# Three mixtures in one kernel: the products with V one item behind, and a spill that is kept in two parts

## The chip, the cores and the metric

One core of a Trainium2 chip runs the whole program. The metric is the device time of one execution in microseconds (us), as the median of the runs given below. Five engines work side by side, each taking its own instructions in the order of its queue: TensorE (PE; its weight loads are listed apart as PEld), VectorE (DVE), ScalarE (ACT), GpSimd (POOL) and SyncE (SP), which here only issues transfers. ACT and POOL issue transfers too.

## The reference, cut to what matters

```
scores = q @ k.T / sqrt(64)                 # 4 batches, 8 heads, 768 tokens, 64 wide
keep   = key among the first 4, or one of the last 128 up to the query
a      = softmax(where(keep, scores, -1e9)) # attention, then  x = a @ v  as 3072 x 512
h      = max(x @ w1, x @ w2, x @ w3)        # first mixture, 768 wide
x2     = h @ w_out                          # 3072 x 512
logits = x2 @ w_gate                        # 8 experts, at most 384 tokens each,
                                            # best (token, expert) bids first
out    = relu(x2 @ W1[e]) @ W2[e]           # second mixture, per token's expert e
```

## The kernel before

The 3072 tokens are cut into eight groups of 384 (half a batch each), numbered 0 to 7. A group's attention is four items (units), one for each pair of heads; item p of group g is written a<g>.<p> below. An item has four steps in class Attn: `load` issues its transfers on SP's queue; `prep` splits k, q and v into two float32r parts, of which one is the value rounded and the other what was left (items of groups 0 and 1 are computed in float32 and need no such split); `score` makes twelve products in PSUM tiles `ps`, copies them into the tile T (ACT, L134) and masks them (DVE, L130 to L137); `soft` takes the maxima (DVE, L141), the exponentials (ACT, L144), and scales T (POOL, L147). Then `pv` transposes T on TensorE (`flip`, L25, into `pt` and `pp`), masks the transposes (DVE, L163), splits them (ACT L176, POOL L177), multiplies with V (TensorE, L181 and L182, into `po`) and writes the item's result tile x (ACT L183, DVE L184; L173 for the float32 items).

The first mixture, class Moe1, works through the groups. `group` first splits a group's four x into the tiles `xh0` to `xh3` and `xl0` to `xl3` (ACT L267, DVE L268; one buffer each), then makes for each of six slices f three times twelve products (L280), takes their maximum into `hm` (ACT L282, DVE L283) and splits this into the parts h and l (ACT L288, DVE L289), which lie in the tile HL. `x2` multiplies these with w_out, 108 products of 260 columns (L305), and writes x2 to memory. Group 0 comes before w_out has been unpacked: its `hm` is written to memory as it is (ACT's queue, L285), and after group 1's x2 `reload` brings each slice back into `hm` (SP's queue, L321), splits it (ACT L323, DVE L324) into HL, and group 0's x2 follows. The eight groups are followed by the routing of the tokens and the second mixture.

Three things set the order of the instructions. First the order in which the program writes them: the lists `order` and `order1` and, from group 2 on, `between(f)`, which emits an item of the next group ahead of slices 0, 1, 3 and 4. Second a scheduler that takes them in order of priority, each as soon as its model of the engines lets it; items of later groups are lifted by 60 instructions (`off`), evictions of PSUM to the front. Third the buffers: x0 to x3, `xh`, `xl`, `pt`, `pp` and `po` have one each, T has three, `mm` and `hm` two. Tiles `st` (two buffers in the pool `conv`) hold words of w_out before they are unpacked in `load_out` (L220 to L228).

Of the kernel before, what the change touches and what calls it, by code (L numbers as in the profile page):

```python
# [19 lines left out]
FT=mybir.dt.float32; FR=mybir.dt.float32r; BF=mybir.dt.bfloat16; I32=mybir.dt.int32; U8=mybir.dt.uint8; U32=mybir.dt.uint32  # L20
AF=mybir.ActivationFunctionType; OP=mybir.AluOpType; AX=mybir.AxisListType
NEG=-8.0e9
def f32(ap): return ap.bitcast(FT)
# [179 lines left out]
class Moe1:  # L203
# [56 lines left out]
    def group(s,xs,spill=None,pool=None,mid=None,between=None):  # L260

        nc=s.nc; main=s.main
        X=[]
        for p in range(4):
            h=main.tile([128,384],FR,name=f"xh{p}",bufs=1); l=main.tile([128,384],FR,name=f"xl{p}",bufs=1)
            with s.tc.high_priority():
                nc.scalar.activation(h,xs[p],AF.Copy)  # L267
                nc.vector.tensor_tensor(l,xs[p],f32(h),op=OP.subtract)  # L268
            X.append((h,l))
        H=[]  # L270
        if s.HL is None and spill is None: s.HL=main.tile([128,12,384],FR,name="HL")
        for f in range(6):
            if between is not None: between(f)
            m=main.tile([128,384],FT,name="hm",bufs=2)
            for i in range(3):
                ps=s.mm.tile([128,512],FT,name="mm")
                n=0
                for p in range(4):
                    for a,b in ((0,0),(0,1),(1,0)):
                        nc.tensor.matmul(ps[:,:384],s.W[i][a][:,p,f*128:(f+1)*128],X[p][b],start=(n==0),stop=(n==11)); n+=1  # L280
                with s.tc.high_priority():
                    if i==0: nc.scalar.activation(m,ps[:,:384],AF.Copy)  # L282
                    else: nc.vector.tensor_tensor(m,ps[:,:384],m,op=OP.max)  # L283
                if mid is not None and (f,i)==s.at: mid()
            if s.HL is None: nc.scalar.dma_start(spill[f],m); continue  # L285
            h,l=(pool.tile([128,384],FR,name=f"h{x}{f}",bufs=1) if pool else s.part(x,f) for x in "hl")
            with s.tc.high_priority():
                nc.scalar.activation(h,m,AF.Copy)  # L288
                nc.vector.tensor_tensor(l,m,f32(h),op=OP.subtract)  # L289
            if spill is not None:  # L290
                for d,x in zip(spill[f],(h,l)): nc.scalar.dma_start(d,f32(x))
            H.append((h,l))
        return H
# [21 lines left out]
                nc.scalar.activation(LG[:,t0+t,:].rearrange("p (u e) -> p u e",u=2),e,AF.Copy)  # L315
            nc.scalar.dma_start(x2d[(t0+t)*128:(t0+t+1)*128,:],o)
    def reload(s,spill):
        nc=s.nc; H=[]
        for f in range(6):
            m=s.main.tile([128,384],FT,name="hm",bufs=2)  # L320
            nc.sync.dma_start(m,spill[f])  # L321
            h,l=s.part("h",f),s.part("l",f)
            nc.scalar.activation(h,m,AF.Copy)  # L323
            nc.vector.tensor_tensor(l,m,f32(h),op=OP.subtract)  # L324
            H.append((h,l))
        return H
    def by_rows(s,spill,t0,x2d,accs,pool):

# [28 lines left out]
class Route:  # L357
# [4 lines left out]
    M=128  # L362
# [261 lines left out]
def attention_mixtures(tc,q,k,v,vs,words,wg,u1,u2,out,off=60,spread=(0,1,3,4),native=8,order='a0 a0 a0 a0 w a1 w a1 w w a1 w w a1 a2',order1='a2 o o o o o o a2 a2',back=1,at=(1,0),s1=300,s2=400,nring=6):  # L624
    nc=tc.nc
    PS=bass.MemoryType.PSUM
    with ExitStack() as ctx:
# [6 lines left out]
        x2d=dram.tile([3072,512],FT,name="x2d")  # L634
        A=Attn(tc,q,k,v,vs,consts,ac,pst,psp,pss,psv,work)
        M=Moe1(tc,words,wg,consts,wpool,main,conv,mm,pst,pss,A.ident)
        M.at=at
        LG=consts.tile([128,24,8],FT,name="LG")
        NG=8; xs={}; cnt={}
        def att(g,p):  # L640
            xs.setdefault(g,[])
            u=A.load(g//2,g%2,p,4*g+p<native); A.prep(u); A.score(u); A.soft(u)
            x=main.tile([128,384],FT,name=f"x{p}")
            A.pv(u,x); xs[g].append(x)
        def lw(f): M.load_w(f)
        def lo(f): M.load_out(f)
        with tc.block(schedule_with_timeline_sim=True):
            A.extra=Spare(main)
            A.kf=[A.zeros([A.extra.tile([128,4,132],FT,tag=f'kf{i}{h}') for h in range(2)]) for i in range(3)]
            def emit(o,p):  # L650
                n=cnt[o]=cnt.get(o,-1)+1
                if o[0]=='a':
                    if p:
                        with tc.high_priority(offset=off): att(int(o[1:]),n)
                    else: att(int(o[1:]),n)
                elif o=='w': lw(n)
                else:
                    A.extra=None; lo(n)
                    if n==5:
                        conv.release()  # L660
                        A.extra=A_("extra",1,side="right"); A.no=('A',)
                        A.kz.append(A.zeros([A.extra.tile([128,4,132],FR,name=f'kz{h}b') for h in range(2)]))
            for o in order.split(): emit(o,False)
            rest=None
            for g in range(NG):
                if g==1:
                    for o in order1.split(): emit(o,True)
                late=list(range(cnt.get(f'a{g+1}',-1)+1,4)) if g+1<NG else []
                def between(f):
                    if f in spread and late: late.pop(0); emit(f'a{g+1}',True)  # L670
                if g<2:
                    while late: between(spread[0])
                d = g>=NG-3
                if g==0: sp=[dram.tile([128,384],FT,name=f"sp{f}") for f in range(6)]
                if g==NG-3: sp2=[[dram.tile([128,384],FT,name=f"sp{f}{x}") for x in "hl"] for f in range(6)]
                if g==NG-1:
                    A.extra.release(); work.release(); ac.release(); psv.release(); pss.release(); psp.release()
                    acc=P("acc",1,space=PS); rc=P("rc",2,space=PS)
                    rt=P("rt",1); rw=P("rw",2); hp=A_("hp",1)
                    r=Route(tc,LG,rt,rw,rc)  # L680
                H6,H=H if g==NG-1 else None,M.group(xs[g],sp if g==0 else sp2 if g==NG-3 else None,hp if g==NG-1 else None,rest,between)
                while late: between(spread[0])
                rest=None
                if d:
                    rest=M.logits(H,3*g,LG)
                    if g==NG-1: r.bids((0,21),True)
                elif g: M.x2(H,3*g,LG,x2d)
                if g==back:
                    M.x2(M.reload(sp),0,LG,x2d)
# [6 lines left out]
        def fet(n):  # L696
            G.append([E.fetch(S[n][0],None if n else T7*128),S[n][1],S[n][0]])
# [22 lines left out]
            P7=[main.tile([128,384],FR,name=f"x{j}") for j in range(3)]  # L720
            for j in range(3): nc.vector.tensor_scalar(P7[j],io,r.q[:,T7+j:T7+j+1],None,op0=OP.is_equal)
        M.x2(H6,T7-3,LG,x2d,256,hp)
        M.by_rows(sp2,T7-6,x2d,acc,hp)
        with tc.high_priority(): fet(0)
        M.x2(H,T7,LG,x2d,256,hp,keep)
        hp.release()
# [62 lines left out]
```

## Time and profile before

| what | value |
|---|---|
| median of 3 runs | 993.31 us (990.75 to 993.98) |
| the profiled execution: its own time | 985.81 us |
| its span, first to last instruction | 984.0 us |
| PE, PEld, DVE, ACT, POOL busy | 937.8, 857.8, 687.8, 533.8, 348.8 us |
| mean granted TensorE clock | 0.977 |

The rows come from one profiled execution, whose own time is 7.5 us under the median of the other runs; a sum of changes is made against it. "Busy" of PE counts pipelined matmuls to their modelled ends, so the weight loads (PEld) show more plainly where TensorE has nothing to do. A granted clock of 1.0 is 2.4 GHz; the lower level is 1.2 GHz, and a value in between is a mix of the two over a stretch.

### The profile page before, as it was taken

How to read it: one execution, taken by the hardware profiler on the slowest of the kernel's cores; microseconds unless marked ns; L12 is line 12 of the kernel's file. 1: busy time of each engine (PE TensorE's matmuls, PEld its weight loads, DVE VectorE, ACT ScalarE, POOL GpSimd, SP SyncE). 2: the span in 40 equal slices, each digit the busy share in tenths (PEclk: the TensorE clock that was granted, in tenths of full speed). 3: DMA queues.
4: the chain of work that ended last, by engine and by line, in shares of the span. 5: the costliest groups of instructions: out<-in, count | busy, mean ns of one | idle time of the engine just before them, and what ended most of it. 6: DMA issues, size and time to landing. Idle time of an engine off the chain costs nothing.

```text
span 984.0 us, 18469 instructions
## 1 busy us (share of the span) xinstructions
PE 937.8 (95%) x6552; PEld 857.8 (87%) x6552; DVE 687.8 (70%) x1807; ACT 533.8 (54%) x1425; POOL 348.8 (35%) x317
## 2 busy tenths in 40 slices
PE   5889999969999999999999999999999999999996
PEld 4568989959999999999999998888888888888895
DVE  3897676687879976776764344879989889873320
ACT  4666664788789777677663211233433434344431
POOL 3578357145555535425434000011113032043331
PEclk8899999989999999999999999999999999999999
DMA  7455121222112112112110002544345352454420
GB/s 226 151 170 172 50 77 64 68 83 88 53 40 78 52 49 73 28 48 81 64 50 12 1 1 76 164 154 130 119 149 174 98 172 99 160 189 154 135 81 32
DMA packets 50541, 95.03 MB, mean 97 GB/s; under 512 B 6704, under 2 KB 20784, under 8 KB 50448
## 3 DMA queue, kind: packets, MB, share of 16 engines
q1 hardware_dynamic: 40560, 71.57, 23.4%
q0 software_dynamic: 3840, 12.45, 3.6%
q10 hardware_dynamic: 6048, 9.83, 2.7%
q8 instruction: 51, 0.84, 0.4%
q14 instruction: 42, 0.34, 0.1%
HBM read 77.84 MB, written 16.12 MB: 95 GB/s over the span
## 4 chain that ended last, share of the span: by engine, by line
PE 75%; DVE 8%; ACT 6%; issue 5%; DMA 4%; POOL 1%; SPq 1%; POOLq 0%; ACTq 0%; DVEq 0%
PE mm L280 28%; PE mm L608 11%; PE acc L601 11%; PE mm L305 7%; PE po L181 3%; PE rc L406 2%; PE pt L25 2%; PE pp L25 2%; PE po L172 2%; PE ps L126 1%; PE ps L127 1%; DMA sa<-in_u_dram 1%; PE ps L123 1%; DVE A_w L163 1%; DVE qs L97 1%
## 5 line engine op out<-in xcount | busy, mean ns | idle before, releaser
L601 PE MATMUL acc<-wbh,HL 128*128 128x512 f32 x384 | 131.1, 398 | 0.0
L177 POOL TENSOR_TENSOR L<-A_w,H 128x768 fp32r<-128x768 f32 x46 | 87.0, 1891 | 101.5 <-ACT H L176 91.1
L283 DVE TENSOR_TENSOR hm<-mm,hm 128x384 f32<-128x384 f32 x96 | 53.3, 555 | 68.6 <-PE mm L280 65.1
L620 POOL DMA_INDIRECT out_dram<-og,idx x24 | 32.2, 1340 | 180.6 <-ACT og L619 177.3
L305 PE MATMUL mm<-woh,HL 128*128 128x260 f32 (+1 forms) x432 | 89.5, 296 | 2.0 <-DVE HL L324 1.1
L552 ACT ACTIVATE wah<-sa 128x512 fp32r<-128x512 f32 x64 | 40.5, 632 | 89.6 <-PE mm L608 72.2
L601 PEld LDWEIGHTS acc<-wbh,HL 128*128 128x128 f32 x384 | 71.5, 188 | 12.8
L552 ACT ACTIVATE wbh<-sb 128x512 fp32r<-128x512 f32 x64 | 40.4, 631 | 74.9 <-PE acc L601 72.0
L601 PE MATMUL acc<-wbl,HL 128*128 128x512 f32 x192 | 76.9, 401 | 0.0
L305 PEld LDWEIGHTS mm<-woh,HL 128*128 128x128 f32 x432 | 72.3, 198 | 3.3 <-DVE HL L324 1.4
L608 PE MATMUL mm<-HL,wah 128*128 128x384 f32 x256 | 68.5, 343 | 0.0
L280 PE MATMUL mm<-xh,w0h 128*128 128x384 f32 x192 | 66.8, 348 | 1.2 <-ACT xh L267 0.6
L280 PE MATMUL mm<-xh,w1h 128*128 128x384 f32 x192 | 66.7, 347 | 0.8 <-ACT hm L282 0.5
L280 PE MATMUL mm<-xl,w0h 128*128 128x384 f32 x192 | 65.5, 341 | 1.9 <-DVE xl L268 1.9
L280 PE MATMUL mm<-xh,w2h 128*128 128x384 f32 x192 | 67.0, 349 | 0.0
L280 PE MATMUL mm<-xh,w1l 128*128 128x384 f32 x192 | 65.5, 341 | 0.0
L280 PE MATMUL mm<-xl,w2h 128*128 128x384 f32 x192 | 65.5, 341 | 0.0
L553 DVE TENSOR_TENSOR wbl<-sb,wbh 128x512 fp32r<-128x512 f32 x64 | 43.9, 688 | 30.7 <-ACT wbh L552 30.7
L280 PE MATMUL mm<-xl,w1h 128*128 128x384 f32 x192 | 65.1, 339 | 0.0
L280 PE MATMUL mm<-xh,w0l 128*128 128x384 f32 x192 | 65.1, 339 | 0.0
L280 PE MATMUL mm<-xh,w2l 128*128 128x384 f32 x192 | 65.1, 339 | 0.0
L612 DVE SCALAR_TENSOR_TENSOR HL<-mm,HL 128x384 fp32r<-128x384 f32 x64 | 35.5, 554 | 40.8 <-ACT HL L611 40.6
(320 smaller groups left out, 2888.3 us busy)
## 6 DMA issues: line engine op xcount, KB each, us to landing
sa<-in_u_dram SPq DMA_DIRECT2D x64, 256.0 KB
sb<-in_u_dram SPq DMA_DIRECT2D x64, 256.0 KB
HL<-in_words_dram SPq DMA_DIRECT2D x18, 512.0 KB
qn<-in_q_dram SPq DMA_DIRECT2D x24, 192.0 KB
x2d<-xo ACTq DMA_DIRECT2D x15, 256.0 KB
kn<-in_k_dram SPq DMA_DIRECT2D x12, 264.0 KB
st<-in_words_dram SPq DMA_DIRECT2D x6, 512.0 KB
vn<-in_v_dram SPq DMA_DIRECT2D x12, 256.0 KB
```

Source lines behind the costliest of these rows:

```text
L25: nc.tensor.transpose(out,x,f32(ident))
L177: nc.gpsimd.tensor_tensor(L,Af,f32(H),op=OP.subtract)
L181: nc.tensor.matmul(po[:,q:q+n],u['VS'][:,blk,128*h:128*h+128],part[:,c:c+n],start=(part is H and j==0),stop=False,skip_group_check=True)
L280: nc.tensor.matmul(ps[:,:384],s.W[i][a][:,p,f*128:(f+1)*128],X[p][b],start=(n==0),stop=(n==11)); n+=1
L283: else: nc.vector.tensor_tensor(m,ps[:,:384],m,op=OP.max)
L305: nc.tensor.matmul(ps[:,:n],H[f][a][:,t*128:(t+1)*128],s.WO[b][:,f,u,c],start=(k==0),stop=(k==17)); k+=1
L552: nc.scalar.activation(h,src,AF.Copy)
L553: (nc.gpsimd if s.n>=6 and nm=="wa" else nc.vector).tensor_tensor(l,src,f32(h),op=OP.subtract)
L601: s.mms.append(nc.tensor.matmul(acc[t],H[f][a][:,t*128:(t+1)*128],W[f][1][b],start=(f==0 and n==0),stop=(f==F-1 and n==2))); n+=1
L608: s.mms.append(nc.tensor.matmul(ps[:,:384],W[f][0][a][:,k,:],X[k][b],start=(n==0),stop=(n==11))); n+=1
L612: nc.vector.scalar_tensor_tensor(l,ps[:,:384],0.0,f32(h),op0=OP.max,op1=OP.subtract)
L620: st=nc.gpsimd.indirect_dma_start(out=s.out,out_offset=bass.IndirectOffsetOnAxis(ap=idx[:,t:t+1],axis=0),in_=o,in_offset=None)
```

## The change

An item's `pv` is no longer emitted with its other steps. `att` appends the item to a list, and `fin(keep, high)` emits the `pv` of the oldest items until `keep` remain. In `order`, one item is kept back among the four of group 0; from group 2's items on, one is kept back after each item, and none after an f or a `load_out` that emits no item. So the `pv` of an item stands behind the load, split, scores and softmax of the next.

Group 0's slices are split as they are made: h and l come from two buffers with the tag `st` of the pool `conv`, and both are written to memory (twelve transfers on ACT's queue instead of six). `reload` only issues twelve transfers on SP's queue: slices 0 to 3 into the tiles `xh0` to `xl3`, slices 4 and 5 into HL.

```diff
-            if s.HL is None: nc.scalar.dma_start(spill[f],m); continue
-            h,l=(pool.tile([128,384],FR,name=f"h{x}{f}",bufs=1) if pool else s.part(x,f) for x in "hl")
+            if s.HL is None: h,l=(s.conv.tile([128,2,384],FR,name="hp",tag="st",bufs=2)[:,x] for x in range(2))
+            else: h,l=(pool.tile([128,384],FR,name=f"h{x}{f}",bufs=1) if pool else s.part(x,f) for x in "hl")
...
     def reload(s,spill):
-        nc=s.nc; H=[]
+        H=[]
         for f in range(6):
-            m=s.main.tile([128,384],FT,name="hm",bufs=2)
-            nc.sync.dma_start(m,spill[f])
-            h,l=s.part("h",f),s.part("l",f)
-            nc.scalar.activation(h,m,AF.Copy)
-            nc.vector.tensor_tensor(l,m,f32(h),op=OP.subtract)
-            H.append((h,l))
+            H.append([s.main.tile([128,384],FR,name=f"x{x}{f}",bufs=1) if f<4 else s.part(x,f) for x in "hl"])
+            for d,x in zip(spill[f],H[f]): s.nc.sync.dma_start(f32(x),d)
         return H
...
+        pend=[]
         def att(g,p):
             xs.setdefault(g,[])
             u=A.load(g//2,g%2,p,4*g+p<native); A.prep(u); A.score(u); A.soft(u)
-            x=main.tile([128,384],FT,name=f"x{p}")
-            A.pv(u,x); xs[g].append(x)
+            pend.append((g,p,u))
+        def fin(keep,high):
+            while len(pend)>keep:
+                g,p,u=pend.pop(0)
+                with tc.high_priority(offset=off) if high else ExitStack():
+                    x=main.tile([128,384],FT,name=f"x{p}")
+                    A.pv(u,x); xs[g].append(x)
...
-            for o in order.split(): emit(o,False)
+            for o in order.split():
+                emit(o,False)
+                fin(int(o[0]=='a' and len(pend)+len(xs.get(0,[]))<4),False)
+            fin(0,False)
...
-                    for o in order1.split(): emit(o,True)
+                    for o in order1.split():
+                        emit(o,True); fin(int(o[0]=='a'),True)
+                    fin(0,True)
...
                 def between(f):
-                    if f in spread and late: late.pop(0); emit(f'a{g+1}',True)
+                    n=int(f in spread and len(late)>0)
+                    if n: late.pop(0); emit(f'a{g+1}',True)
+                    fin(n,True)
...
-                if g==0: sp=[dram.tile([128,384],FT,name=f"sp{f}") for f in range(6)]
-                if g==NG-3: sp2=[[dram.tile([128,384],FT,name=f"sp{f}{x}") for x in "hl"] for f in range(6)]
+                if g in (0,NG-3): sp=[[dram.tile([128,384],FT,name=f"sp{g}{f}{x}") for x in "hl"] for f in range(6)]
...
-                H6,H=H if g==NG-1 else None,M.group(xs[g],sp if g==0 else sp2 if g==NG-3 else None,hp if g==NG-1 else None,rest,between)
+                H6,H=H if g==NG-1 else None,M.group(xs[g],sp if g in (0,NG-3) else None,hp if g==NG-1 else None,rest,between)
                 while late: between(spread[0])
+                fin(0,True)
```

## Rows read from the trace of the kernel before

**Rows 1.** Stages: PE, PEld, DVE, ACT, POOL busy (instructions), clock, DMA share, GB/s.

```profile
0.00:64.00 64.00, 46.68 (x190) 31.24 (x190) 43.39 (x103) 38.83 (x136) 34.53 (x47) 0.87 0.61 189
64.00:125.00 61.00, 60.48 (x340) 53.93 (x341) 46.78 (x90) 38.54 (x120) 39.94 (x40) 0.97 0.35 115
...
199.00:236.50 37.50, 29.61 (x193) 27.42 (x194) 30.91 (x52) 33.04 (x99) 19.38 (x14) 0.82 0.28 85
236.50:300.00 63.50, 62.85 (x422) 61.88 (x420) 50.91 (x104) 51.93 (x156) 31.73 (x30) 1.00 0.18 52
300.00:557.00 257.00, 253.94 (x1692) 249.32 (x1692) 177.99 (x350) 173.32 (x495) 109.60 (x92) 1.00 0.16 50
557.00:984.00 427.00, 412.30 (x3230) 364.46 (x3227) 286.90 (x1005) 149.04 (x292) 81.05 (x68) 0.99 0.37 120
```

**Rows 2.** TensorE in order of time, 199 to 239 us: start, us, instructions, [idle before].

```profile
205.89 0.59 PE L126 MATMUL ps<-kh_x,qs 128*128 128x260 f32 x1 [2.00 <-DVE T_w L135]
...
206.49 0.42 PE L305 MATMUL mm<-woh,HL 128*128 128x260 f32 x1
...
208.70 0.80 PE L305 MATMUL mm<-woh,HL 128*128 128x260 f32 x2 [1.14 <-DVE HL L324]
...
217.83 0.39 PE L126 MATMUL ps<-kh_w,qs 128*128 128x260 f32 x1 [1.97 <-DVE T_w L135]
...
221.13 0.90 PE L25 MATMUL pp<-ident,T_w 128*128 128x128 f32 x3 [1.24 <-DVE A_w L163]
...
222.27 0.42 PE L305 MATMUL mm<-woh,HL 128*128 128x260 f32 x1
...
228.15 0.28 PE L305 MATMUL mm<-woh,HL 128*128 128x260 f32 x1
228.27 0.28 PE L305 MATMUL mm<-wol,HL 128*128 128x260 f32 x1
...
236.48 0.34 PE L280 MATMUL mm<-xh,w0h 128*128 128x384 f32 x1
```

**Rows 3.** The reload's instructions: count, ns least/median/most, first and last start.

```profile
L323 ACT ACTIVATE HL<-hm x6: 506/516/526, 196.3 to 213.2; 128x384 fp32r<-128x384 f32 x6
L324 DVE TENSOR_TENSOR HL<-hm,HL x6: 551/556/2194, 198.8 to 213.8; 128x384 fp32r<-128x384 f32 x6
...
L285 ACTq DMA_DIRECT2D sp<-hm x6: 326/326/341, 72.6 to 122.6; - x6
L321 SPq DMA_DIRECT2D hm<-sp x6: 320/327/334, 175.3 to 210.8; - x6
```

**Rows 4.** ScalarE in order of time, 200 to 300 us.

```profile
213.21 0.53 ACT L323 ACTIVATE HL<-hm 128x384 fp32r<-128x384 f32 x1 [1.60 <-DMA hm<-sp]
...
236.98 0.51 ACT L267 ACTIVATE xh<-x 128x384 fp32r<-128x384 f32 x1
...
293.84 1.77 ACT L267 ACTIVATE xh<-x 128x384 fp32r<-128x384 f32 x4
```

**Rows 5.** VectorE and GpSimd in order of time, 207 to 221 us.

```profile
207.41 3.35 DVE L324 TENSOR_TENSOR HL<-hm,HL 128x384 fp32r<-128x384 f32 x2
...
215.66 1.91 DVE L95 TENSOR_TENSOR kz0b<-kn,kh_x 64x528 fp32r<-64x528 f32 x1 [0.36 <-ACT kh_x L94]
...
220.12 0.96 DVE L163 TENSOR_TENSOR A_w<-pp,ul 128x768 f32<-128x768 f32 x1
...
208.19 2.15 POOL L177 TENSOR_TENSOR L<-A_w,H 128x768 fp32r<-128x768 f32 x1
```

**Rows 6.** TensorE in order of time, 23 to 65 us.

```profile
23.50 0.85 PE L25 MATMUL pt<-ident,T_w 128*128 128x128 f32 x3
...
64.52 0.44 PE L280 MATMUL mm<-xl,w0h 128*128 128x384 f32 x1 [1.10 <-DVE xl L268]
```

**Rows 7.** A transfer of w_out's words on SP, and ScalarE's first use of it.

```profile
135.86 0.33 SPq L220 DMA_DIRECT2D st<-in_words_dram  x1
...
140.22 0.68 ACT L226 ACTIVATE st<-st 128x512 int32<-128x512 uint32 x1 [2.26 <-DMA st<-in_words_dram]
```

More of the change, by code (lines that the diff above doesn't have):

```diff
@@ L722, in attention_mixtures @@
         M.x2(H6,T7-3,LG,x2d,256,hp)
-        M.by_rows(sp2,T7-6,x2d,acc,hp)
+        M.by_rows(sp,T7-6,x2d,acc,hp)
         with tc.high_priority(): fet(0)
```

## The prediction

> **What bounds the kernel now.** I read the shares by stage first, then TensorE in order of time where a stage is poor, then the instructions that end its waits, and last the queues of ScalarE, VectorE and GpSimd there. The reader should look in the first view for a stage in which weight loads (the second pair) fill less than the stage at a granted clock under 1.0. Up to 64 us TensorE is fed by transfers and by unpacking: loads fill 31.24 of 64 us. From 236.5 to 557 us it is nearly full: 61.88 of 63.5 and 249.32 of 257 us, at clock 1.00, so only 1.62 + 7.68 = 9.3 us are free there. The routing and the second mixture behind 557 us are not touched. One stage in the middle is poor: 199 to 236.5 us, 27.42 of 37.5 us at clock 0.82 [rows 1].
>
> What that stage loses: 37.5 - 27.42 = 10.1 us without a load. A mean of 0.82 between the levels 1.0 and 0.5 means 0.36 of the stage, 13.5 us, at 1.2 GHz; with the stage's own busy share of 0.73 that is 9.9 us of loads, which would have taken 4.9 us less at 2.4 GHz. Together 15.0 us, so the stage's work is 22.5 us at full clock. This is my scale for what a cure can give.
>
> In order of time one sees why. Group 0's x2, which works on the reloaded slices, starts at 206.49, waits 1.14 us for a reloaded slice's l at 208.70, and its second product begins only at 222.27, because TensorE's queue holds scores and transposes of items in between that wait for VectorE: 2.00, 1.97 and 1.24 us [rows 2]. VectorE was late because the reload's six subtractions lie there, one of 2.19 us against a median of 0.556 [rows 3], two of them with a span of 3.35 us, and because a split of k for a later item (1.91 us) comes ahead of the mask at 220.12 that frees `pp` [rows 5]. ScalarE itself waited 1.60 us for a transfer of the reload [rows 4]. Group 2's products follow at 236.48 [rows 2].
>
> **The reload.** Removed from the poor stage: six ACT copies of 0.516 us, 3.1 us, and six DVE subtractions, five at the median and one of 2.194, 5.0 us [rows 3]. ACT is the fuller of the two, 33.04 us of 37.5 [rows 1]; 29.9 us remain. If the stage stayed as full of ACT work as it is (0.88), it would last 34.0 us and the gain is 3.5; if ACT becomes gapless, 29.9 us and 7.6; if only TensorE counted, 22.5 us and 15.0. Nothing excludes 0, if another chain ends as late. I take 7.5: group 0's x2 no longer needs ACT and DVE, so TensorE has 108 products that are ready while the items' chains run, and a part of ACT's work here belongs to group 3's items and may slip. This also gives back clock, which falls here where TensorE waited and rises again once products run.
>
> Added in its place: twelve SP issues for six, 0.327 us each [rows 3]. Eight go into `xh`/`xl`, free once group 1's products end, and have group 1's whole x2 (108 products at 0.12 us, the distance of two such products, 13 us [rows 2]) to land. The four of slices 4 and 5 overwrite HL, so they wait for the last reads of group 1's x2. A transfer of the reload issued at 210.8 let ACT start at 213.21, 2.4 us [rows 3, 4]; four issues take 1.3 us, so slice 5 stands 3.7 us behind that last read. The first twelve products of group 0's x2 cover 1.4 us: up to 2.3 us uncovered, unless scores fill it. Queued behind these issues on SP are the next item's k and q. At the end, group 2's splits (0.51 us on ACT [rows 4], 0.556 on DVE as any such subtraction [rows 3]) must wait for `xh0` to be read for the last time, 15 products or 1.8 us before x2 ends; 1.1 us fits under that if both queues are free, and costs up to 1.1 us if not. I take +1.0 for both (0 to 3.4).
>
> **The split at group 0.** Six ACT copies (3.1 us), six more ACT issues of 0.326 us (2.0) and six subtractions (3.3) move to between 72.6 and 122.6 us [rows 3]. In that stage ACT has 61 - 38.54 = 22.5 us free and DVE 14.2, and TensorE is the full engine (PE 60.48 of 61) [rows 1]. So I take +0.5, with 0 and the whole 8.4 us as ends, the latter if no cover holds. Slots of `st` are taken until the last spill has landed, about 122.6 + 1.1 + 0.3 + 2.4 = 126.4 us; a load of w_out's words and its first use are 4.4 us apart [rows 7], so the second word comes at about 131 us, while group 0's and 1's x2 lie behind 175 us (the reload's first issue) [rows 3]. No cost, as long as six unpackings fit in 44 us.
>
> **One item behind.** No instruction is added; the queues' order changes. ACT, DVE and POOL work on the next item's scores and softmax ahead of the old item's splits, so the last item of a group has its T earlier and TensorE's transposes are asked for later. In the steady part only 9.3 us can be won [rows 1]. Group 3's four splits run as one piece of 1.77 us at 293.84 [rows 4]: all four x had been waiting, and 13 us of x2 follow before they are needed. So being later costs nothing at first. I take -1.5 (from -9.3 to +5.5, the latter if each of five boundaries lost the 1.10 us that TensorE waited for an x's l at 64.52 [rows 6]). At the start the fourth item ends group 0's wait there; a `pv` has two masks of 0.96 us on DVE [rows 5], and putting one `pv` behind the next scores moves the fourth item by at most that, 1.9 us, either way. The transposes of the first item already start at 23.50 [rows 6] among the others' scores; I take -1.0.
>
> **The sum**: -7.5 + 1.0 + 0.5 - 1.5 - 1.0 = -8.5 us. The profiled execution took 985.81 us, so 977.3; the shown median is 993.31, 7.5 us above it, and on that scale the forecast is 984.8 us. I use the median's scale below. 0.3%, 3 us, is about what a measurement here can tell from no change.
>
> **The rivals.** (B) The stall only moves. Group 2 needs the fourth x as well, whose split starts at 236.98 [rows 4], and this chain runs through ACT and DVE, not through the reload. Then the stage shortens by 3.5 us (ACT stays as full as it is), 1.5 of it are paid for the late slices, nothing else comes: -2, 991.3 us. For it: ACT at 0.88; against it: ACT and DVE lose 8 us of work ahead of that chain.
>
> (C) The whole stall goes: 13.5 of 15 us, the two new waits find scores as cover, and the other terms as above: -15.5, 977.8 us. For it: the 108 products that are no longer tied to VectorE. Against it: masks and splits of the items remain.
>
> (D) Slower, in group 0's stage. A slice's second spill waits on ACT's queue for the subtraction on DVE; behind it stand the eviction of the next slice's first product and the items' exponentials, and `mm` has only two buffers, so TensorE stops. GpSimd is busy 39.94 of 61 us there, more than in the poor stage (19.38 of 37.5) [rows 1], and the subtraction of 2.19 us ran while GpSimd's own, at 208.19 for 2.15 us, did [rows 5]. At 2.2 us a slice, six cost 13.2 us in place of 0.5: +4.2, 997.5 us. It decides from 1.5 us a slice on (six of them undo the other 9.0 us). Against it: ACT has 22.5 us free, and TensorE has items' float32 products to run.
>
> The Trainium skill, SBUF — State Buffer, in "SBUF: two separate sides", says that VectorE and GpSimd take an exclusive lock on a shared port pair and that an operation of VectorE with two SBUF inputs is blocked while a GpSimd operation that reads SBUF runs; this speaks for (D). The trace agrees with the 2.19 us against 0.556 [rows 3, 5]; by the rule alone, each of the six would meet GpSimd with its busy share of 0.65 and wait half of 2.15 us, an estimate of 4.2 us on DVE, and were none of that hidden the sum would be -4.3 us instead of -8.5.
>
> (E) Emitting `pv` later does nothing, because the scheduler goes by readiness: its two terms fall away, -6.0, 987.3 us.
>
> **Chances.** The forecast (980 to 989) 0.47; E 0.08; B 0.20; C 0.12; D 0.13. B lies about the 3 us limit: 0.04 of it is faster, 0.14 the same, 0.02 slower; 0.01 of D is the same. So faster 0.71, same 0.15, slower 0.14. For 8 in 10 I reach to 975, which leaves out a third of C, and to 996, which leaves out most of D.
>
> **What would show it.** Right: no ACT or DVE instruction of the reload between 195 and 215 us; group 0's x2 in one run behind group 1's, at clock 1.00; group 2's first product 6 to 8 us earlier; group 0's last spill not later than some 124 us. Wrong: TensorE waiting on a transfer into HL for over 2 us, or on `xl` behind that x2 (B); `mm` waits of TensorE between 72 and 123 us that end on ACT, with subtractions over 1 us (D); more free time of loads between 236.5 and 557 us than 9.3 us, ended by an x or its split, which would mean that the later `pv` is late.

## The result: 0.55% slower, and the profile after

Timed side by side, the kernel before took 992.86 us (median of 14 runs, 990.49 to 995.64) and the changed one 998.94 us (14 runs, 994.35 to 1004.99): ratio 1.0055, 95% interval 1.0041 to 1.0069, so about 5.5 us slower by this ratio (the two medians lie 6.1 us apart). The forecast was 984.8 us with a range of 975 to 996: wrong way, and outside the range. The profiled execution took 994.35 us, span 992.6 us, mean clock 0.984.

Line numbers of the changed kernel: the split is L288 (ScalarE) and L289 (VectorE), its spill L291, the reload L321; the products (L280), x2 (L305) and the items (L75 to L184) keep theirs.

The first view is the shares by stage of the kernel after (columns as in [rows 1]), cut at the same four times for every kernel below; the second is the same view of the kernel before.

```profile
120.00:150.00 30.00, 24.40 (x136) 21.83 (x135) 22.41 (x42) 21.75 (x62) 17.07 (x13) 0.83 0.36 116
150.00:190.00 40.00, 39.97 (x266) 39.68 (x265) 31.18 (x67) 25.65 (x67) 17.25 (x18) 1.00 0.24 72
190.00:240.00 50.00, 45.46 (x345) 44.00 (x345) 41.02 (x60) 40.25 (x131) 20.80 (x17) 0.97 0.34 110
240.00:560.00 320.00, 309.91 (x2065) 303.24 (x2065) 230.10 (x449) 220.44 (x634) 138.15 (x118) 1.00 0.16 48
```

```profile
120.00:150.00 30.00, 28.26 (x179) 25.68 (x178) 22.85 (x45) 20.32 (x57) 15.50 (x14) 1.00 0.21 70
150.00:190.00 40.00, 40.00 (x279) 39.83 (x278) 25.55 (x61) 23.06 (x59) 17.96 (x17) 1.00 0.24 74
190.00:240.00 50.00, 41.77 (x284) 39.23 (x283) 40.75 (x69) 45.21 (x145) 22.47 (x16) 0.86 0.29 88
240.00:560.00 320.00, 316.29 (x2109) 310.01 (x2108) 228.57 (x452) 222.88 (x634) 139.74 (x120) 1.00 0.16 49
```

My measure for all kernels is **lost TensorE time**: the length of a stretch minus its weight loads times the granted clock, added up over pieces of 5 us. It counts empty time and time at the lower clock alike. Before and after it is 44.7 and 40.6 us up to 120 us; 4.3 and 11.4 in 120 to 150; 0.2 and 0.3 in 150 to 190; 15.3 and 7.5 in 190 to 240; 10.0 and 16.8 in 240 to 560. So the change wins 4.1, loses 7.1, wins 7.8 and loses 6.8: 2.1 us worse at 560 us. The reader should see the second and third of these in the rows: loads of 25.68 fall to 21.83 with the clock down to 0.83, and then loads of 39.23 rise to 44.00 with the clock up from 0.86 to 0.97.

The last product of group 7 starts at 602.0 us after, 598.8 before, 3.2 us apart. The rest of the two spans' 8.6 us lies behind it, where both kernels have the same instructions in the same order on every engine. From that product to the end of the span took 382.6 to 387.8 us in all kernels of those series of runs in which before's median was 985 to 986 us, and 390.6 to 396.4 where it was 992 to 993; the profile before (385.2) belongs to the first kind, after's (390.6) to the second. I therefore compare each kernel's time within its series, and profiles by group 7's last product. What stays open is that the times differ by 5.5 us and the profiles, up to there, by 3.2.

TensorE in order of time, after:

```profile
128.60 0.55 PE L25 MATMUL pt<-ident,wol 128*128 128x128 f32 x3 [2.06 <-POOL wol L147]
...
130.70 0.69 PE L280 MATMUL mm<-xh,w0h 128*128 128x384 f32 x1 [1.23 <-ACT xh L267]
...
133.03 0.90 PE L25 MATMUL pp<-ident,wol 128*128 128x128 f32 x3 [1.32 <-DVE A_w L163]
...
136.21 1.12 PE L25 MATMUL ps<-ident,cA 128*128 128x128 f32 x4 [1.00 <-POOL cA L228]
...
209.93 0.29 PE L305 MATMUL mm<-woh,xh 128*128 128x260 f32 x1
...
231.85 0.28 PE L305 MATMUL mm<-woh,HL 128*128 128x260 f32 x1
...
232.69 0.34 PE L280 MATMUL mm<-xh,w0h 128*128 128x384 f32 x1
...
233.81 0.44 PE L280 MATMUL mm<-xl,w0h 128*128 128x384 f32 x1 [0.25 <-DVE xl L268]
...
337.77 0.45 PE L280 MATMUL mm<-xh,w1h 128*128 128x384 f32 x1 [1.48 <-DVE hm L283]
```

Four waits of 5.6 us together follow each other within 10 us, for group 2's first item (its probabilities `wol`, its mask `A_w`), for the split of group 1's fourth x, and for a word of w_out; all these come due close together here. Group 0's x2 then runs from 209.93 to 231.85, and group 2's products begin at 232.69 in place of 236.48 [rows 2]. SP's queue (issues in order of time) shows why w_out is later, and how the reload goes:

```profile
124.75 1.48 SPq L220 DMA_DIRECT2D st<-in_words_dram  x2
...
186.01 0.33 SPq L321 DMA_DIRECT2D xl<-sp00l  x1
...
208.71 0.33 SPq L321 DMA_DIRECT2D HL<-sp04h  x1
...
210.08 0.38 SPq L321 DMA_DIRECT2D HL<-sp05l  x1
```

Eight transfers go out while group 1's x2 runs, and four, whose places in HL had been read for the last time, as group 0's x2 begins (208.7 to 210.1 us); no product waits for them. The same groups of instructions, first of the kernel before (`st`), then of the one after (`st` and `hp`; ns least, median, most, then first and last start):

```profile
L220 SPq DMA_DIRECT2D st<-in_words_dram x6: 327/356/585, 22.0 to 161.2; - x6
```

```profile
L220 SPq DMA_DIRECT2D st<-in_words_dram x6: 327/328/328, 124.8 to 153.7; - x6
...
L288 ACT ACTIVATE hp<-hm x6: 508/519/529, 68.9 to 122.3; 128x384 fp32r<-128x384 f32 x6
L289 DVE TENSOR_TENSOR hp<-hm,hp x6: 544/891/1466, 69.6 to 123.4; 128x384 fp32r<-128x384 f32 x6
```

w_out's first word is asked for 103 us later than before, and VectorE begins to unpack it 4.9 us later (130.7 us in place of 125.8); SP waited 3.7 us in front of it for group 0's last spilled slice, with the next item's v, k and q behind.

### The profile page after: what moved, and what is told of

It is laid out like the page before. It is cut to its first block, busy times and chain, and to the rows that moved or that the text cites. A ratio compares the mean times of both kernels' runs of the same rounds, so it can differ in the third digit from the quotient of the medians.

```text
span 992.6 us, 18471 instructions
## 1 busy us (share of the span) xinstructions
PE 933.8 (94%) x6552; PEld 853.0 (86%) x6552; DVE 698.7 (70%) x1807; ACT 532.5 (54%) x1425; POOL 348.9 (35%) x317
## 4 chain that ended last, share of the span: by engine, by line
PE 66%; DVE 13%; ACT 8%; issue 7%; DMA 3%; POOL 2%; SPq 1%; POOLq 0%; DVEq 0%; ACTq 0%
PE mm L280 23%; PE mm L604 11%; PE acc L597 11%; PE mm L305 5%; PE po L181 3%; PE rc L402 2%; DVE qs L97 2%; PE pt L25 2%; PE po L172 1%; PE ps L123 1%; DMA sa<-in_u_dram 1%; ACT T_w L144 1%; PE pp L25 1%; DVE A_w L163 1%; DVE m L141 1%
## 5 line engine op out<-in xcount | busy, mean ns | idle before, releaser
L305 PE MATMUL mm<-woh,HL 128*128 128x260 f32 (+1 forms) x384 | 76.8, 288 | 3.4 <-ACT xo L307 1.4
L280 PE MATMUL mm<-xh,w1h 128*128 128x384 f32 x192 | 67.3, 351 | 4.2 <-DVE hm L283 3.4
L280 PE MATMUL mm<-xh,w0h 128*128 128x384 f32 x192 | 66.9, 349 | 2.9 <-ACT xh L267 2.0
L280 PE MATMUL mm<-xh,w2h 128*128 128x384 f32 x192 | 66.6, 347 | 0.9 <-DVE hm L283 0.7
L280 PE MATMUL mm<-xl,w0h 128*128 128x384 f32 x192 | 65.8, 343 | 0.3 <-DVE xl L268 0.3
L305 PEld LDWEIGHTS mm<-woh,HL 128*128 128x128 f32 x384 | 61.5, 188 | 4.7 <-DVE HL L289 1.9
L280 PE MATMUL mm<-xl,w2h 128*128 128x384 f32 x192 | 65.5, 341 | 0.0
L280 PE MATMUL mm<-xl,w1h 128*128 128x384 f32 x192 | 65.4, 341 | 0.0
L280 PE MATMUL mm<-xh,w0l 128*128 128x384 f32 x192 | 65.3, 340 | 0.0
L280 PE MATMUL mm<-xh,w2l 128*128 128x384 f32 x192 | 65.1, 339 | 0.0
L280 PE MATMUL mm<-xh,w1l 128*128 128x384 f32 x192 | 64.9, 338 | 0.0
L608 DVE SCALAR_TENSOR_TENSOR HL<-mm,HL 128x384 fp32r<-128x384 f32 x64 | 35.4, 553 | 41.3 <-ACT HL L607 41.1
```

Source lines behind the costliest of these rows:

```text
L305: nc.tensor.matmul(ps[:,:n],H[f][a][:,t*128:(t+1)*128],s.WO[b][:,f,u,c],start=(k==0),stop=(k==17)); k+=1
L608: nc.vector.scalar_tensor_tensor(l,ps[:,:384],0.0,f32(h),op0=OP.max,op1=OP.subtract)
```

## The experiments

Theory 1 at the start: emitting pv later costs the time, in the steady part. Theory 2: holding `st` makes w_out late and costs it at 120 to 150 us. All 20 kernels, the two above and 18 more, stand in one table. Ratio: to the kernel before in the same series of runs, with its 95% interval. "End": start of group 7's last product. The other columns: lost TensorE time in us. "Head start" is the number `off`, 60 in both kernels: the priority that items get in the planned order.

| kernel | ratio | end | to 120 | 120-150 | 190-240 | 240-560 | to 560 |
|---|---|---|---|---|---|---|---|
| before | 1 | 598.8 | 44.7 | 4.3 | 15.3 | 10.0 | 74.5 |
| before, head start 55 | 1.0050 (1.0032-1.0068) | 604.8 | 44.1 | 4.3 | 15.4 | 14.2 | 78.2 |
| before, 65 | 1.0064 (1.0039-1.0089) | 602.8 | 41.1 | 3.9 | 14.4 | 17.2 | 76.8 |
| after | 1.0055 (1.0041-1.0069) | 602.0 | 40.6 | 11.4 | 7.5 | 16.8 | 76.6 |
| after, 55 | 1.0080 (1.0054-1.0106) | 602.6 | 41.0 | 10.8 | 6.3 | 18.8 | 77.3 |
| after, 65 | 1.0116 (1.0089-1.0142) | 608.9 | 41.8 | 12.5 | 7.5 | 21.4 | 83.4 |
| spill and reload alone | 1.0102 (1.0077-1.0127) | 604.0 | 42.0 | 11.2 | 8.1 | 14.7 | 77.3 |
| later pv alone | 1.0102 (1.0082-1.0122) | 608.1 | 44.1 | 4.3 | 14.4 | 18.6 | 83.0 |
| after, pv later in front only | 1.0108 (1.0092-1.0124) | 606.1 | 42.5 | 11.5 | 8.5 | 17.5 | 81.1 |
| after, pv later from group 2 on | 1.0089 (1.0073-1.0106) | 607.3 | 44.0 | 13.0 | 7.3 | 18.1 | 82.6 |
| spill elsewhere, pv as before | 1.0105 (1.0069-1.0140) | 610.1 | 44.2 | 8.1 | 10.0 | 22.4 | 85.3 |
| the same, 55 | 1.0098 (1.0080-1.0116) | 608.4 | 46.3 | 5.9 | 10.3 | 20.5 | 83.7 |
| the same, 65 | 1.0043 (1.0028-1.0059) | 600.1 | 40.6 | 8.4 | 10.8 | 15.3 | 75.7 |
| after, spill elsewhere | 1.0044 (1.0019-1.0068) | 602.7 | 45.0 | 8.0 | 4.6 | 19.7 | 77.4 |
| the same, 55 | 1.0039 (1.0022-1.0056) | 604.0 | 44.4 | 9.0 | 4.5 | 21.0 | 79.0 |
| the same, 65 | 1.0009 (0.9995-1.0024) | 597.1 | 42.7 | 9.0 | 4.3 | 17.2 | 73.3 |
| after, elsewhere, l on GpSimd | 1.0034 (1.0019-1.0049) | 603.4 | 45.0 | 8.6 | 6.5 | 19.0 | 79.3 |
| the same, 65 | 1.0111 (1.0093-1.0130) | 611.1 | 46.3 | 8.9 | 6.2 | 24.5 | 86.2 |
| after, elsewhere, 65, w_out first | 0.9995 (0.9978-1.0011) | 596.4 | 41.5 | 1.9 | 13.0 | 14.0 | 73.1 |
| the same, half of w_out first | 1.0033 (1.0012-1.0055) | 600.6 | 43.5 | 1.6 | 12.5 | 16.2 | 76.7 |

### Each part alone

Spill and reload alone: the kernel before with `reload` and the spill of the change. Later pv alone: the change with before's spill and reload.

```
-            if s.HL is None: nc.scalar.dma_start(spill[f],m); continue
+            if s.HL is None: h,l=(s.conv.tile([128,2,384],FR,name="hp",tag="st",bufs=2)[:,x] for x in range(2))
...
+                fin(n,True)
```

> The spill and reload of the change alone; every pv stays with its item. Theory 1 (the later pv costs the time): the poor stage at 190 to 240 us loses 7 to 8 us less of TensorE than before, the rest stays as before, so 6 to 9 us faster than before (ratio 0.991 to 0.994). Theory 2 (the spill's hold on the tiles st makes w_out's words late and costs 7 us at 120 to 150 us): the gain is eaten, within 3 us of before, with TensorE short of work at 120 to 150 us as in the changed kernel.

> The later pv alone, everywhere; spill and reload as before. Theory 1: 4 us gained up to 120 us and lost again where group 1 starts, 7 us lost from group 2 on, and the stall of the reload at 200 to 222 us stays: 5 to 12 us slower than before (ratio 1.005 to 1.012). Theory 2: no loss at 120 to 150 us, 4 us faster to 3 us slower.

Both are 1.0% slower than before, and each alone is worse than the two together (1.0055). Theory 1 (the later pv costs it all) gave the range for the later pv alone rightly (1.005 to 1.012) and missed the other kernel (0.991 to 0.994); theory 2 (the hold on `st` costs it all) missed both. As whole accounts both fall. The stages agree with parts of both: the loss at 120 to 150 comes with the spill (11.2 against 4.3) and not with the later pv (4.3), and so does the cure at 190 to 240 (8.1 against 14.4). The shares of "spill and reload alone":

```profile
120.00:150.00 30.00, 24.68 (x137) 21.61 (x136) 20.72 (x42) 21.40 (x62) 14.26 (x13) 0.83 0.35 111
...
190.00:240.00 50.00, 44.75 (x338) 42.98 (x336) 38.60 (x66) 44.37 (x143) 22.38 (x16) 0.97 0.34 109
```

and of "later pv alone", where the reload's stage is as poor as before, at the same 0.86:

```profile
190.00:240.00 50.00, 41.69 (x291) 39.90 (x291) 35.91 (x61) 40.95 (x130) 20.77 (x17) 0.86 0.28 88
```

The later pv in front only, and from group 2's items on:

```
-                        emit(o,True); fin(int(o[0]=='a'),True)
+                        emit(o,True); fin(0,True)
...
-                fin(int(o[0]=='a' and len(pend)+len(xs.get(0,[]))<4),False)
+                fin(0,False)
```

> The changed kernel, but the later pv is kept only among the four items of group 0; from group 2's items in order1 on each pv follows its own softmax again. Theory 1: the 7 us lost between 240 and 560 us come back, so 5 to 8 us faster than the changed kernel and about 1 to 5 us faster than before. Theory 2: as slow as the changed kernel, give or take 2 us.

> The changed kernel, but the later pv is kept only from group 2's items on; the four items of group 0 have theirs at once. Theory 1: the 4 us won up to 120 us go, but they were lost again at group 1's start, so as slow as the changed kernel, within 3 us; the 7 us loss between 240 and 560 us stays. Theory 2: the same at 120 to 150 us, and no loss from 240 us on.

Neither half is the culprit: 1.0108 and 1.0089. All four have more loss in 240 to 560 us than before, 14.7 to 18.6 against 10.0, even those whose items are emitted there exactly as before. Theory 1 had expected the kernel with the later pv in front only to be 5 to 8 us faster than the changed one, and theory 2 the other to lose nothing from 240 us on; neither came. That led to theory 3: the order is planned, every edit draws a new one, and before's is a good draw.

### Another place for the spill, and other orders of the same work

Group 0's h goes into the buffer of `xo`, unused until w_out is unpacked, and l in place of `hm`; `st` stays free. And the kernel before with nothing changed but the head start.

```
-h,l=(s.conv.tile([128,2,384],FR,name="hp",tag="st",bufs=2)[:,x] for x in range(2))
+h,l=main.tile([128,520],FT,name="xo",bufs=1)[:,:384].bitcast(FR),m.bitcast(FR)
...
-off=60
+off=55
```

> The spill and the reload of after on the kernel before, but group 0's h lies in the buffer of xo, which nothing uses then, and its l takes the place of hm; the two st buffers are not touched, so w_out's first two words can be loaded as early as before. Theory 3 (two terms): the hold on st costs 7 us at 120 to 150, and any new order of the queues costs 5 to 8 us in 240 to 560; the cure of the reload gives 7. Then lost TensorE time in 120 to 150 falls back from 11.4 to some 4 to 6 us, 190 to 240 stays at 7 to 8, 240 to 560 loses 15 or more against 10, and the time is 992 to 996 us beside 992 to 993 of before, 5 to 8 us under the variant with st. Rival (the hold costs nothing, the loss at 120 to 150 has another cause): 11 us are lost there again, and the time stays at 1000.

> The whole change with the same place for group 0's h and l. Theory 3: 120 to 150 loses 4 to 6 us in place of 11.4, so 5 to 7 us under after: 992 to 994. Rival: as after, 999.

> The kernel before with one number changed, the head start that items get in the planned order, 60 to 55 instructions: the same work in an order that differs in a few per cent of its places. Theory 3 (the order of before happens to be a good one, and most others cost 5 to 8 us in the steady part): 996 to 1000 us. Rival (the later loss belongs to the change itself): within 3 us of before, 990 to 996.

> As the kernel with 55, with 65. Theory 3: 996 to 1000 us. Rival: 990 to 996.

The two neutral orders are 0.50 and 0.64% slower, as much as the whole change. Up to 240 us they lose no more than before, and the one with 65 loses 3.6 us less up to 120; their extra loss is in the steady part, as in this row (before, 65), with 304.54 us of loads in place of 310.01:

```profile
240.00:560.00 320.00, 310.53 (x2058) 304.54 (x2057) 229.60 (x441) 218.00 (x624) 135.81 (x119) 0.99 0.16 48
```

This part of theory 3 is shown, by two orders. The hold on `st` is only half of the extra loss at 120 to 150: 8.1 and 8.0 us remain of 11.2 and 11.4, beside 4.3 before, where I had expected 4 to 6. The times were worse than expected too: 1.0105 where theory 3 said at most 996 us beside 992 to 993, and 1.0044 where it said 992 to 994. With the later pv and `st` free, the loss at 190 to 240 falls to 4.6.

Three orders of each, to part the change from the luck:

> The whole change with the items' head start at 55 in place of 60. Two neutral changes of that number made the kernel before 0.50 and 0.64% slower, so its own order is a lucky one. Theory 3: the change has a gain of its own of about nothing to 5 us, and after's 0.55% is no more than the loss of that luck; then after with 55 scatters about 1.004, from 1.000 to 1.008 of before, and a kernel of after is not slower than the kernel of before with the same number (1.005). Rival (the change costs time by itself, about 5 us): 1.009 to 1.013.

> The whole change with the head start at 65. Theory 3: 1.000 to 1.008 of before, not over the 1.0064 that the kernel before has with 65. Rival (the change costs time by itself): 1.010 to 1.014.

> The whole change with group 0's h in xo's buffer and l in hm's, head start 55. In that variant with 60, 4.6 us of TensorE time were lost in 190 to 240 (15.3 before) and 19.7 in 240 to 560 (10.0 before). Theory 3: the first is kept with any order (4 to 9), the second scatters between 12 and 20, so 0.995 to 1.006 of before. Rival: the later loss stays at 18 to 20 whatever the number, 1.004 to 1.010.

> The whole change with group 0's h in xo's buffer and l in hm's, head start 65. Theory 3: 4 to 9 us lost in 190 to 240, 12 to 20 in 240 to 560, 0.995 to 1.006 of before. Rival (the later loss stays at 18 to 20 whatever the number): 1.004 to 1.010.

Mean over head starts 55, 60 and 65: before +0.38%, after +0.84%, after with the spill elsewhere +0.31% (of before at 60). Theory 3's bound, that after is no slower than before with the same number, is missed: 1.0080 against 1.0050, 1.0116 against 1.0064, the latter in the range of the rival that the change costs time by itself (1.010 to 1.014). So of after's mean, 0.38% is what a new order costs before as well, and about 0.46% is the change's own; with `st` free, that is gone (0.31 against 0.38%). Three orders each, which differ by up to 0.64% among themselves, make these means rough; that the spill elsewhere is faster holds for each of the three (0.11, 0.41, 1.07%). The profiles say where this gain and this loss lie: up to 240 us the three with the spill elsewhere lose 57.3 us in the mean and the three of before 62.7, and from 240 to 560 us 19.3 against 13.8, so the gain at the front is gone by 560 us.

### Without the later pv, and the subtractions on GpSimd

The spill elsewhere without the later pv, two more orders; and the whole change, spill elsewhere, with group 0's six subtractions moved:

```
-                nc.vector.tensor_tensor(l,m,f32(h),op=OP.subtract)
+                (nc.gpsimd if s.HL is None else nc.vector).tensor_tensor(l,m,f32(h),op=OP.subtract)
```

> The new spill and reload without the later products with V, group 0's h and l outside st, head start 55. In 240 to 560 us, the eight kernels with later products there lost 16.8 to 21.3 us of TensorE time, mean 18.8; six without lost 10.0 to 22.4, mean 16. If the later products cost by themselves (2 to 4 us), this and its sister with 65 lose 12 to 16 there and stand at 0.994 to 1.001 of before; if it is the order alone, they scatter between 10 and 22 with a mean near 18, 1.000 to 1.010.

> The same as the kernel with 55, head start 65. Later products cost by themselves: 12 to 16 us lost in 240 to 560, 0.994 to 1.001 of before. The order alone: anywhere between 10 and 22 us, 1.000 to 1.010.

> The whole change, group 0's h and l outside st, and l's six subtractions on GpSimd in place of VectorE, head start 60. At 124 to 136 us VectorE is busy 11.8 of 12 us and TensorE waits for its mask. If the subtractions at that boundary make the rest of the loss, 120 to 150 us lose 4 to 6 us in place of 8.0, and the time is 3 us or more under the kernel with them on VectorE (1.0044): 0.998 to 1.002. If not, 7 to 9 us are lost there again, 1.002 to 1.008.

> The same with the head start at 65, where the kernel with the subtractions on VectorE took 1.0009 of before and lost 9.0 us at 120 to 150. If the subtractions make it: 4 to 6 us, 0.994 to 0.999 of before, faster than both kernels. If not: 8 to 9 us, 0.999 to 1.006.

Without the later pv 20.5 and 15.3 us are lost in 240 to 560, within what all new orders lose: the later pv can't be told from the order there. Over the whole kernel it is better on top of the new reload in all four pairs: 1.0102 to 1.0055 with `st`, and elsewhere 1.0105 to 1.0044, 1.0098 to 1.0039, 1.0043 to 1.0009. With the spill elsewhere its gain is at 190 to 240, 10.0 to 10.8 against 4.3 to 4.6.

The subtractions were not the rest of the boundary's loss: 8.6 and 8.9 us. With head start 65 the time, 1.0111, lies outside both ranges expected, with 24.5 us lost in 240 to 560. The shares of 120 to 150 us, first with them on VectorE, then on GpSimd (head start 60):

```profile
120.00:150.00 30.00, 27.70 (x153) 25.29 (x152) 23.49 (x45) 20.56 (x62) 15.77 (x14) 0.89 0.24 76
```

```profile
120.00:150.00 30.00, 26.75 (x152) 23.96 (x151) 25.25 (x45) 20.97 (x63) 20.33 (x18) 0.89 0.30 97
```

```profile
L289 POOL TENSOR_TENSOR hm<-hm,xo x6: 1011/1014/1026, 73.6 to 124.5; 128x384 fp32r<-128x384 f32 x6
```

GpSimd got 4.6 us more and VectorE did not get less, but 1.8 us more. Little of this can be laid to the move itself: of the six subtractions only the last, at 124.5 us, lies in this stage, and in the second kernel one more word of w_out is unpacked in it (four on VectorE in place of three). Over 60 to 150 us, where all six lie, VectorE's busy time fell by 0.4 us (70.7 to 70.4), though the six had taken 4.7 us of it; what filled the rest was not followed up.

### What stands in front of the mask

What VectorE did there (after, spill elsewhere, 65), with TensorE's wait and GpSimd below it:

```profile
123.81 2.13 DVE L268 TENSOR_TENSOR xl<-x,xh 128x384 fp32r<-128x384 f32 x2
...
126.73 1.54 DVE L97 TENSOR_TENSOR qs<-qn,qs 64x384 fp32r<-64x384 f32 x1
128.30 0.56 DVE L289 TENSOR_TENSOR hm<-hm,xo 128x384 fp32r<-128x384 f32 x1
128.89 1.26 DVE L95 TENSOR_TENSOR kz<-kn,kh_w 64x396 fp32r<-64x396 f32 x1
...
131.24 0.55 DVE L97 TENSOR_TENSOR qs<-qn,qs 64x384 fp32r<-64x384 f32 x1
...
132.43 0.95 DVE L163 TENSOR_TENSOR A_w<-pp,ul 128x768 f32<-128x768 f32 x1
...
133.44 0.90 PE L25 MATMUL pp<-ident,wol 128*128 128x128 f32 x3 [1.84 <-DVE A_w L163]
...
123.98 1.54 POOL L228 TENSOR_TENSOR cA<-cA,st 128x512 int32<-128x512 int32 x1 [1.65 <-DVE cA L227]
126.12 1.74 POOL L147 TENSOR_TENSOR wol<-wol,l 128x792 f32<-128x792 f32 x1 [0.60 <-DVE l L146]
128.44 1.28 POOL L109 TENSOR_TENSOR vsp<-vn,vsp 128x384 fp32r<-128x384 f32 x1 [0.58 <-ACT vsp L108]
```

The splits of q and k belong to a group 2 item; each that meets a GpSimd operation takes 1.26 or 1.54 us, where the same two took 0.52 us (at 125.96, begun 0.16 us ahead of a GpSimd operation) and 0.55 us (131.24, beside an idle GpSimd). Behind them comes the mask of group 2's first item, whose transposes stand ahead of group 1's remaining products on TensorE: it waits 1.84 us for this mask, and the last x's own split comes later still (134.18). To test this, the one item of group 2 that `order1` has ahead of w_out's six slices was emitted behind all six of them, and in a second kernel behind the third. The first of these edits:

```
-order1='a2 o o o o o o a2 a2'
+order1='o o o o o o a2 a2 a2'
```

> The whole change, group 0's h and l outside st, head start 65, and group 2's second to fourth items emitted behind the six slices of w_out in place of one ahead and two behind. If the splits of the second item, which stand ahead of the mask on VectorE, make TensorE's 2 us wait and the fall of the clock behind it, 120 to 150 us lose 4 to 6 us in place of 9.0, with no granted clock under 0.9 in the stretch; with the later stages as in the kernel with one item ahead (1.0009 of before), 0.996 to 0.998. If the wait has another cause, 8 to 9 us are lost there again. By the scatter that every new order had so far (0.001 to 0.012 over before), 1.001 to 1.008.

> The same with the second item behind the third slice of w_out. If its splits make the wait: 4 to 6 us lost at 120 to 150, 0.996 to 0.999 of before. If not: 8 to 9 us, 1.001 to 1.008.

The shares with w_out first:

```profile
120.00:150.00 30.00, 30.00 (x192) 28.12 (x190) 18.22 (x35) 15.14 (x37) 19.72 (x18) 1.00 0.20 65
150.00:190.00 40.00, 37.76 (x266) 37.28 (x266) 28.06 (x68) 30.47 (x88) 8.46 (x8) 1.00 0.26 80
190.00:240.00 50.00, 42.69 (x298) 40.47 (x297) 34.80 (x63) 43.53 (x136) 26.30 (x22) 0.90 0.30 95
```

The boundary's loss is gone, 1.9 and 1.6 us, less than before's 4.3 and at clock 1.00 (4 to 6 us were expected): that this item came due there was its cause. That it was the item's splits on VectorE, and not the rest of its work, is read from the rows above and was not tested by itself. But the cure goes with it: 13.0 and 12.5 us are lost at 190 to 240 in place of 4.3, though the new reload is there. My reading, argued and not tested, is that the items' work on ScalarE and VectorE has to be done between 120 and 240 us, and stalls TensorE at the one end or the other. The kernel with the lowest ratio, w_out first, is level with before (0.9995, 0.9978 to 1.0011), short of the 0.996 to 0.998 expected, and the second (1.0033) lies in the range for another cause (1.001 to 1.008); none was measurably faster.

## Why the prediction was wrong

**The reload** was right in its size: -7.5 forecast, 15.3 to 7.5 measured. The four kernels with the old reload lose 14.4 to 15.4 us there, those with the new one 4.3 to 10.8, but for the two that emit items later there (12.5 and 13.0). From group 1's last product to group 2's first it took 45.3 us in place of 55.7. The new waits, +1.0, cost about nothing (0.25 us at 233.81). Two signs were off: group 0's x2 did not go in one run (22 us for 108 products), and group 2 began 3.8 us earlier, not 6 to 8, because group 1 ended 6.6 us later (187.4 against 180.8). One reading behind this term was wrong. Group 0's x2 did not start at 206.49 before, but with this row:

```profile
199.94 0.39 PE L305 MATMUL mm<-woh,HL 128*128 128x260 f32 x1 [0.53 <-ACT xo L307]
```

The last of group 1's 108 products starts at 197.47 us; twelve of group 0's run from 199.94 and 24 more from 206.49 to 215, so two of its six results were summed side by side, and at 222.27 the third began, not the second. The waits that the prediction names stand as they are.

**The split at group 0** was the term that failed: +0.5 taken, 7.1 us more lost at 120 to 150, inside the stated 0 to 8.4 but by another way. I argued with the free time of ScalarE and VectorE between 64 and 125 us, and there it holds: nothing more is lost up to 120, although the subtractions took 0.891 us in the median. The price stands at the boundary to group 1, where group 1's last x, group 2's first item and w_out's slices come due together and VectorE is the full engine (3.88 and 3.94 of 4 us even before, below). "No cost, as long as six unpackings fit in 44 us" looked only at when w_out is needed (they do fit, starting at 124.8); it did not ask what else comes due in the stretch into which they are moved. Holding `st` is 2 to 4 us of the stage's loss; the rest goes when one item of group 2 is emitted later, as the two last kernels show.

With the spill elsewhere, the clock makes almost the whole difference to before that is left there (8.0 against 4.3). Two stretches in pieces of 4 us, with TensorE's waits in them, before and then after with the spill elsewhere:

```profile
128.00:132.00 4.00, 3.44 (x21) 2.54 (x19) 3.88 (x7) 3.33 (x9) 2.76 (x2) 1.00 0.37 105
132.00:136.00 4.00, 2.82 (x19) 2.35 (x20) 3.94 (x9) 4.00 (x17) 1.48 (x2) 1.00 0.45 175
136.00:140.00 4.00, 4.00 (x25) 4.00 (x26) 1.56 (x4) 1.97 (x5) 4.00 (x3) 1.00 0.42 135
...
132.13 1.06 PE L255 MATMUL ps<-wg,xo 128*128 128x8 f32 x8 [0.69 <-ACT xo L252]
...
135.18 0.56 PE L181 MATMUL po<-H,vsp 128*128 128x256 f32 x3 [0.91 <-ACT wgt L256]
```

```profile
132.00:136.00 4.00, 2.06 (x17) 1.79 (x18) 3.91 (x7) 1.88 (x5) 1.52 (x2) 1.00 0.48 149
136.00:140.00 4.00, 4.00 (x20) 3.95 (x19) 2.97 (x7) 4.00 (x17) 1.86 (x1) 0.55 0.42 137
140.00:144.00 4.00, 4.00 (x15) 4.00 (x15) 0.38 (x3) 1.49 (x5) 1.83 (x1) 0.59 0.00 0
...
134.86 0.55 PE L25 MATMUL pp<-ident,wol 128*128 128x128 f32 x3 [1.94 <-DVE A_w L163]
```

Before, TensorE waited 0.69 and 0.91 us there and stayed at 2.4 GHz; with a wait of 0.36 and one of 1.94 us the next 8 us ran mostly at 1.2 GHz, which cost 4 x 0.45 + 4 x 0.41 = 3.4 us. In the kernel after, the clock fell to 0.80 in 128 to 132 us, where the first two of its four waits end (3.3 us), and was 0.50 from 132 to 140 us.

**One item behind**: the -1.0 at the start came out as -4.1, but the later pv isn't shown to be its cause: alone it gives 0.6 (44.1 against 44.7 to 120 us), the new spill alone 2.7 (42.0), and before with head start 65 gives 3.6 (41.1) with neither. The boundary took it back, since group 1's fourth x came no earlier (its split at 130.13 us, 129.82 before). The -1.5 in the steady part is the second step that failed: 6.8 us more lost from 240 to 560, past the upper end of +5.5. I had read [rows 1] as a stage in which "only 9.3 us can be won" and priced the waits that an item's lateness adds. What I left out is that any edit makes a new order of every queue, and that 10.0 us is a low draw: two neutral orders of before lose 14.2 and 17.2 there, and the 17 changed kernels 14.0 to 24.5. The waits themselves are small and spread: the longest after, 1.48 us at 337.77, is for `hm`, behind these:

```profile
334.11 2.13 DVE L97 TENSOR_TENSOR qs<-qn,qs 64x384 fp32r<-64x384 f32 x1
336.27 0.98 DVE L141 TENSOR_REDUCE m<-T_x 128x6 f32<-128x792 f32 x1
337.16 0.55 DVE L283 TENSOR_TENSOR hm<-mm,hm 128x384 f32<-128x384 f32 x1
...
333.96 1.86 POOL L177 TENSOR_TENSOR L<-A_w,H 128x768 fp32r<-128x768 f32 x1 [2.68 <-ACT H L176]
```

A split of q that met GpSimd's subtraction took 2.13 us, and the eviction that frees `mm` stood behind it. That is what I had named as the sign ("more free time of loads than 9.3 us"), except that its ends are mostly evictions and masks (an x ends 0.6 of TensorE's 9.9 us of waits there).

**The rivals.** D had the sign, and at 997.5 us a time near the one measured, at the wrong place: nothing more is lost up to 120 us, and TensorE's only wait for `mm` between 72 and 123 us is 0.9 us and ends on VectorE. B, C and E do not describe it. The rule behind D's second paragraph, in the Trainium skill, SBUF — State Buffer, "SBUF: two separate sides" (a GpSimd operation that reads SBUF locks out VectorE's with two SBUF inputs), agrees with these rows (2.13, 1.54 and 1.26 us when begun during a GpSimd operation, 0.52 and 0.55 when not); here it matters for splits of q, k and x.

What stays open: how much of the extra loss in 240 to 560 us, 18.8 us in the mean of twelve orders with later pv there against 16.5 in eight without, is the later pv's and not the draw's; and why holding `st` costs 0.5%, 5 us, in the times when the profiles show 2 to 4 us of it at the boundary.

## What to carry to other kernels

Where the order of the queues is planned, an edit is timed together with a new order: change a neutral number of the old and the new kernel first, and compare the families, not two single draws. A stall is a place at which the work of other engines comes due; curing what ended it is worth what those engines need not do elsewhere, so add up the whole stretch in which their work can move (here 120 to 240 us: 19.8 us lost before, 19.2 after, 12.7 after with the spill elsewhere). Memory borrowed from a buffer that is "free for now" moves every transfer that would have used it.

## Unexpected in the hardware

In the rows above, splits of q and k on VectorE took 1.26 to 2.13 us when they began while a GpSimd operation ran, and 0.52 to 0.55 when they began beside an idle GpSimd. Waits of 0.36 and 1.94 us were followed by 1.2 GHz on TensorE where two of 0.69 and 0.91 us at the same place had not been. And the part behind group 7's products, the same instructions in the same order, took 382.6 to 387.8 us in some series of runs and 390.6 to 396.4 in others; no run shows why.
